# Leaving out semaphore waits that other waits imply, in a planned attention-and-MLP decode kernel

## The chip, the cores and the metric

The kernel runs on one core of a Trainium2 chip. The core has a matrix engine (PE, with a weight-load lane shown as PEld), a vector engine (DVE), an activation engine (ACT), a general-purpose engine (POOL) and a synchronising engine (SP), which here only issues DMA transfers. Each engine works through its own program in order, and the engines meet through semaphores: an instruction can add to a semaphore when it is done, and an instruction can be held until a semaphore has reached a value. The metric is device time in microseconds (us); smaller is better.

## The reference, cut to what matters

Eight sequences decode one token each. The kernel computes a gated sum of an attention branch over the last 2048 cached positions and an MLP branch.

```python
# x: (8, 1, 576); k_cache, v_cache: (8, 16, 8192, 128); all bfloat16
W = 2048
q = (x @ wq).reshape(8, 1, 32, 128).transpose(0, 2, 1, 3)   # 32 query heads
k = repeat(k_cache[:, :, -W:, :], 2, axis=1)                # 16 kv heads, 2 queries each
v = repeat(v_cache[:, :, -W:, :], 2, axis=1)
p = softmax(einsum("bhqd,bhkd->bhqk", q, k) * 128 ** -0.5)
a = einsum("bhqk,bhkd->bhqd", p, v).transpose(0, 2, 1, 3).reshape(8, 1, 4096) @ wo
y = layernorm(x)                                            # no scale, no shift
b = gelu(y @ w1 + b1) @ w2 + b2                             # 576 -> 4608 -> 576
g = sigmoid((x * gate_w).sum(-1, keepdims=True))
out = g * a + (1 - g) * b                                   # (8, 1, 576)
```

## The kernel before

Nearly all the bytes are the two cache windows. They are cut into 32 K units and 32 V units of 2 MB each (one of 8 groups of two kv heads, and a quarter of that group). All big transfers are issued by SP in one fixed order into nine slots of on-chip memory: the two projection weights wq and w1, five K units, then K and V units in turn, with V trailing K by five or six units and one 1.15 MB piece of wo after every eighth V unit. The last in that order are K31, then V26 to V31, the last piece of wo, the bias b2 and the four chunks of w2, the last of them in three pieces. A transfer into a slot waits until the work that read the slot before is done.

What is done with the pieces:

- A K unit is transposed in two halves by DVE (L653). After each half PE adds eight matmuls into four banks of scores (L667; L663 lays down a mask first, once in a group). POOL copies the query columns for it into a block-diagonal operand (L646, names that begin with "qr").
- After a group's fourth K unit comes its softmax. DVE takes the row maximum (L598), moves three of its quarters to the first 32 partitions (L601), combines them (L602, L603, L604) and writes the negated maximum to all four quarters (L607). ACT takes four exponentials (L612), DVE transposes each (L617), sums (L620) and spreads the sums (L621); PE adds them over partitions (L622), and DVE takes the reciprocal (L623) and multiplies in the gate (L629).
- A V unit is 16 matmuls (L690). ACT copies the result out (L696), PE selects the wanted blocks with four fp32 matmuls (L701), and after every second V unit ACT copies the pair out (L711) and POOL scales it (L719).
- After every eighth V unit PE gathers the rows (L734), ACT copies them (L738), and PE multiplies with wo (L552). The products with b2 and w2 go through L552 too. All of L552 adds up in one bank. At the end DVE (L779) and ACT (L780) each copy half of that bank out, and SP and ACT issue the two stores (L782).

The order of the work on each engine is settled before anything runs. Every operation is an `_Op` with a list `deps` of operations that it must wait for. `_Plan.schedule` (from L62) simulates the engines with assumed costs, and from the result writes down one order for each engine; each operation gets its place `pos` in it and its planned start and end, `t0` and `t1`. At the end it adds a wait between neighbouring POOL operations of different kinds (L116 to L121), numbers the transfers on each DMA semaphore, and numbers those operations that somebody waits for (`milestone`).

`_Plan.emit` (from L141) then writes one engine's program. For each dependency of an operation it calls `wait_ge` (L153), unless this engine has already waited for the same semaphore at that value or a higher one; that is the only waiver there is. One wait travels on the instruction itself: the first one called for. Each further wait becomes an instruction of its own ahead of it, holding one or two waits, and shows in the profile as line L153 on the engine's queue (DVEq, ACTq and so on). An operation that has a milestone adds one to its engine's semaphore when it is done.

Of the kernel before, what the change touches and what calls it, by code (L numbers as in the profile page):

```python
# [12 lines left out]
ENGS = ("sp", "act", "pool", "dve", "pe")  # L13
# [25 lines left out]
class _Plan:  # L39
# [22 lines left out]
    def schedule(self):  # L62
        n = len(self.all)
        done = [False] * n
        eng_free = {e: 0.0 for e in ENGS}
        dma_free = 0.0
        remaining = set(range(n))
        npred = [0] * n
        succ = [[] for _ in range(n)]
        for op in self.all:  # L70
            preds = set(d.idx for d in op.deps) | set(d.idx for d in op.after)
            npred[op.idx] = len(preds)
            for p in preds:
                succ[p].append(op.idx)
        ready = [i for i in range(n) if npred[i] == 0]
        count = 0
        while ready:
            best = None
            best_key = None
            for i in ready:  # L80
                op = self.all[i]
                r = 0.0
                for d in op.deps:
                    r = max(r, d.t1 + self.SEM_LAT)
                for d in op.after:
                    r = max(r, d.t0)
                est = max(eng_free[op.eng], r)
                key = (est - 0.2 * op.prio, -op.prio, i)
                if best_key is None or key < best_key:
                    best_key = key  # L90
                    best = i
            op = self.all[best]
            ready.remove(best)
            est = max([eng_free[op.eng]] + [d.t1 + self.SEM_LAT for d in op.deps] + [d.t0 for d in op.after])
            op.t0 = est
            if op.is_dma:
                eng_free[op.eng] = est + op.cost
                if op.nbytes < 65536:
                    op.t1 = est + 0.4 + self.DMA_LAT
                else:  # L100
                    start = max(est + 0.4, dma_free)
                    dma_free = start + op.nbytes / self.DMA_BW
                    op.t1 = dma_free + self.DMA_LAT
            else:
                op.t1 = est + op.cost
                eng_free[op.eng] = op.t1
            op.pos = len(self.order[op.eng])
            self.order[op.eng].append(op)
            done[best] = True
            count += 1  # L110
            for s_ in succ[best]:
                npred[s_] -= 1
                if npred[s_] == 0:
                    ready.append(s_)
        assert count == n, "dependency cycle in plan"
        self.makespan = max(op.t1 for op in self.all)  # L116
        prev = None
        for op in self.order["pool"]:
            narrow = op.name.startswith("qr")
            if prev is not None and narrow != prev.name.startswith("qr"):  # L120
                op.deps.append(prev)  # L121
            prev = op
        cnts = {}
        for e in ENGS:
            for op in self.order[e]:
                if op.is_dma:
                    cnts[op.dma_sem] = cnts.get(op.dma_sem, 0) + 1
                    op.dma_val = 16 * cnts[op.dma_sem]
        needed = set()
        for op in self.all:  # L130
            for d in op.deps:
                if not d.is_dma:
                    needed.add(d.idx)
        for e in ENGS:
            c = 0
            for op in self.order[e]:
                if op.idx in needed:
                    c += 1
                    op.milestone = c
# [713 lines left out]
```

## Time and profile before

| | us |
|---|---|
| median of three runs | 369.81 |
| the three runs | 368.82 to 369.83 |
| the profiled execution: device time | 369.34 |
| the profiled execution: span from first to last instruction | 367.6 |
| PE busy | 268.4 (73%) |
| DVE busy | 212.1 (58%) |
| ACT busy | 48.8 (13%) |
| POOL busy | 42.3 (12%) |

All times of the argument are taken from the one profiled execution. What lies around its span is 369.34 - 367.6 = 1.74 us. Busy shares are means over the whole span. The chain that ended last, which the profile follows back from the last instruction, tells which work set the end at each moment; in it, time called "issue" is time in which an engine waited for nothing that the profile shows, and a name with a q (DVEq, ACTq, POOLq) is an engine's queue handling an instruction that does no arithmetic.

### The profile page before, as it was taken

To read this page: it belongs to the slowest core of one execution; us is meant where nothing else is said; L and a number is where in the kernel's file an instruction comes from. 1 tells how busy PE (TensorE), PEld (TensorE's weight loads), DVE (VectorE), ACT (ScalarE), POOL (GpSimd) and SP (SyncE) were. 2 spreads that over 40 slices of the span, in tenths; PEclk is the share of its full clock that TensorE was granted. 3 is DMA by queue.
4 is the path that set the end of the run, shared out by engine and by line. 5 is a ranking of instruction groups with operands and counts; after the bars stand their busy time and mean duration, and the time that the engine had idled before them with its cause. 6 is when DMAs were issued, how large, how long until landed. Compare 5 with 4: busy or idle time off the path is not lost.

```text
span 367.6 us, 4620 instructions
## 1 busy us (share of the span) xinstructions
PE 268.4 (73%) x1869; PEld 132.4 (36%) x1869; DVE 212.1 (58%) x254; ACT 48.8 (13%) x122; POOL 42.3 (12%) x166
## 2 busy tenths in 40 slices
PE   0349984699598498874986488875987489684887
PEld 0339431244244243332432243322433244232454
DVE  0804599699687764459744754469644874464000
ACT  1010000201300310003000300003000310004110
POOL 8020011012012001010111010010111000000000
PEclk9999998599799878887898878887888788985558
DMA  8999999999999999999999999999999999999993
GB/s 345 428 417 428 430 431 431 431 428 430 428 433 430 425 436 430 428 431 431 431 435 430 420 437 431 427 431 435 428 426 430 437 429 427 426 430 437 421 428 158
DMA packets 11341, 154.62 MB, mean 421 GB/s; under 512 B 1292, under 2 KB 1332, under 8 KB 1976
## 3 DMA queue, kind: packets, MB, share of 16 engines
q1 hardware_dynamic: 11264, 154.29, 98.4%
q8 instruction: 15, 0.25, 0.2%
q10 hardware_dynamic: 56, 0.03, 0.0%
q14 instruction: 6, 0.05, 0.0%
HBM read 154.31 MB, written 0.01 MB: 420 GB/s over the span
## 4 chain that ended last, share of the span: by engine, by line
DMA 58%; PE 20%; DVE 16%; issue 4%; ACT 1%; POOL 1%; SPq 0%; POOLq 0%; DVEq 0%; ACTq 0%
DMA arena<-in_A_k_cache_dram 51%; DVE arena L653 12%; PE ps L667 9%; DMA arena<-in_B_w_dram 7%; PE ps L552 2%; PE ps L509 2%; DVE arena L598 2%; PE ps L690 2%; PE ps L701 2%; PE ps L663 1%; DVE arena L617 1%; PE ps L511 1%; DVE arena L607 0%; DVE arena L601 0%; ACT arena L696 0%
## 5 line engine op out<-in xcount | busy, mean ns | idle before, releaser
L653 DVE STREAM_TRANSPOSE arena<-arena 128x2048 f32<-128x2048 f32 x64 | 145.1, 2296 | 71.8 <-DMA arena<-in_A_k_cache_dram 68.2
L667 PE MATMUL ps<-arena 128*128 128x512 bf16 x512 | 151.7, 453 | 17.2 <-DVE arena L653 17.1
L667 PEld LDWEIGHTS ps<-arena 128*128 128x128 bf16 x512 | 53.8, 112 | 107.0 <-issue 41.1
L646 POOL COPY arena<-arena 32x32 bf16<-32x32 bf16 x128 | 26.0, 203 | 215.4 <-PE ps L667 200.8
L701 PE MATMUL ps<-arena 128*128 128x8 f32 x256 | 37.2, 272 | 15.4 <-ACT arena L696 15.4
L701 PEld LDWEIGHTS ps<-arena 128*128 128x128 f32 x256 | 35.9, 214 | 29.3 <-ACT arena L696 28.0
L696 ACT ACTIVATE arena<-ps 128x512 f32<-128x512 f32 x32 | 19.1, 598 | 191.6 <-PE ps L690 191.6
L663 PE MATMUL ps<-arena 128*128 128x512 bf16 x32 | 14.9, 621 | 33.7 <-DVE arena L617 29.0
L690 PE MATMUL ps<-arena 128*32 128x512 bf16 x512 | 37.1, 413 | 0.7 <-ACT arena L711 0.7
L598 DVE TENSOR_REDUCE arena<-ps 128x1 f32<-128x2048 f32 x8 | 18.3, 2282 | 18.0 <-PE ps L667 18.0
L612 ACT ACTIVATE arena<-ps,arena 128x512 bf16<-128x512 f32 x32 | 21.6, 686 | 41.8 <-DVE arena L607 41.8
L617 DVE STREAM_TRANSPOSE arena<-arena 128x512 bf16<-128x512 bf16 x32 | 19.8, 674 | 0.9 <-ACT arena L612 0.9
L719 POOL TENSOR_TENSOR arena<-arena 128x128 bf16<-128x128 f32 x16 | 8.1, 509 | 91.5 <-ACT arena L711 90.7
L690 PEld LDWEIGHTS ps<-arena 128*32 128x32 bf16 x512 | 11.3, 100 | 18.8 <-issue 12.5
L663 PEld LDWEIGHTS ps<-arena 128*128 128x128 bf16 x32 | 3.5, 127 | 39.4 <-DVE arena L617 35.0
L779 DVE CAST arena<-ps 8x288 bf16<-8x288 f32 x1 | 0.4, 445 | 29.1 <-PE ps L552 29.1
L509 PE MATMUL ps<-arena 128*128 128x8 bf16 x144 | 10.9, 201 | 4.7 <-DMA arena<-in_B_w_dram 4.7
L552 PE MATMUL ps<-arena 128*8 128x288 bf16 (+1 forms) x140 | 12.7, 348 | 1.3 <-ACT arena L738 1.3
L509 PEld LDWEIGHTS ps<-arena 128*128 128x128 bf16 x144 | 10.8, 159 | 5.2 <-DMA arena<-in_B_w_dram 5.2
L623 DVE RECIPROCAL arena<-ps 128x32 f32<-128x32 f32 x8 | 2.9, 358 | 13.4 <-PE ps L622 13.4
L422 PE MATMUL ps<-arena 8*128 8x8 bf16 x8 | 0.5, 167 | 13.5 <-DVE arena L395 9.8
L552 PEld LDWEIGHTS ps<-arena 128*8 128x8 bf16 (+1 forms) x140 | 6.8, 99 | 5.2 <-ACT arena L738 1.8
(88 smaller groups left out, 97.7 us busy)
## 6 DMA issues: line engine op xcount, KB each, us to landing
arena<-in_A_k_cache_dram SPq DMA_DIRECT2D x32, 2048.0 KB, 35.2
arena<-in_A_v_cache_dram SPq DMA_DIRECT2D x32, 2048.0 KB, 36.5
arena<-in_B_w_dram SPq DMA_DIRECT2D x1, 4608.0 KB, 24.2
arena<-in_A_wo_dram SPq DMA_DIRECT2D x4, 1152.0 KB, 35.8
arena<-in_A_wq_dram SPq DMA_DIRECT2D x1, 4096.0 KB, 12.9
arena<-in_B_w_dram SPq DMA_DIRECT2D x3, 1296.0 KB, 33.6
arena<-in_B_w_dram SPq DMA_DIRECT2D x2, 576.0 KB, 28.5
arena<-in_A_wq_dram SPq DMA_DIRECT2D x1, 512.0 KB, 3.3
```

What stands on the lines that cost most here:

```text
L509: ins = e.matmul(out_, lhsT, yT[:, kt, :], start=(kt == 0), stop=False)
L552: ins = e.matmul(ps[32 * j:32 * j + 8, BK_ACC, 0:JN], lhsT, rhs[:, JN * j:JN * j + JN], start=False, stop=True, skip_group_check=True, til ...
L598: mx = add("dve", lambda e: e.tensor_reduce(out=k(MX), in_=ps[:, 0:4, :].rearrange("p a n -> p (a n)"), axis=AXL.X, op=ALU.max), deps=[qk_ ...
L612: return e.activation(out=Pm[:, 512 * c:512 * c + 512], in_=ps[:, c, :], func=ACTF.Exp, bias=k(NB), scale=SCALE, accum_out=k(SUM + c))
L617: pts.append(add("dve", (lambda c=c: lambda e: e.transpose(bass.AP(arena, offset=aoffs("PT") + (g % 2) * 2048 + 128 * c, ap=[[AST, 128], [ ...
L646: return e.tensor_copy(dst, src)
L653: tr = add("dve", (lambda h=h, kb=kb: lambda e: e.transpose(bass.AP(arena_f, offset=foffs("KT") + kb * 2048, ap=[[AST // 2, 128], [1, 2048]]),
L663: mm = e.matmul(ps[:, rc, :], maskL, maskR, start=True, stop=False)
L667: mm = e.matmul(ps[:, rc, :], qbd[:, ub, 2 * h + ee, :], rhs, start=False, stop=(q == 3 and h == 1 and ee == 1))
L690: mm = e.matmul(ps[32 * t:32 * t + 32, BK_OS[i % 2], :], PT[:, g % 2, q, 32 * r4:32 * r4 + 32], slot(s)[:, 512 * r4:512 * r4 + 512], start ...
L696: o_ev[i] = add("act", lambda e: e.activation(out=osb[:, i % 2, :], in_=ps[:, BK_OS[i % 2], :], func=ACTF.Copy), deps=[prev] + ([o_sel[i - ...
L701: mm = e.matmul(ps[:, BK_OS[i % 2], 0:8], osb[:, i % 2, 128 * r:128 * r + 128], i32[:, 8 * r:8 * r + 8], start=(r == 0), stop=(r == 3), sk ...
```

## The change

After the orders are fixed, a new pass goes through the engines' programs and works out for each operation what is known to be done by the time it starts. For every engine and every DMA semaphore it keeps the highest position known to be complete: what the engine's own earlier waits have shown, and what the operations waited for had themselves waited for. A dependency that this knowledge covers already, or that another dependency of the same operation covers, is dropped from `deps`. The ones kept stand in order of planned end, latest first. An engine's own earlier operations count as complete only where a wait has shown it.

The orders of the engines' instructions stay as they were; nothing but waits and semaphore increments differs. In the built programs the instructions that only wait go from 89 to 45 on PE, 49 to 24 on DVE, 35 to 9 on ACT, 30 to 26 on POOL and 35 to 3 on SP (131 fewer in all; each count has the few of the start and the end in it). As fewer operations are waited for, the instructions that increment a semaphore go from 160 to 124 on PE, 258 to 162 on DVE, 98 to 97 on ACT and 166 to 52 on POOL. Because the kept waits are sorted, the wait that travels on the instruction can be another one than before: ahead of some V units it was the wait for the transfer, with the wait for ACT ahead of it, and now it is the wait for ACT, with the transfer's ahead.

```diff
         needed = set()   # in schedule(); the lines below stand ahead of this one
+        key = lambda d: ("dma", d.dma_sem) if d.is_dma else ("eng", d.eng)
+        val = lambda d: d.dma_val if d.is_dma else d.pos + 1
+        last = {e: {} for e in ENGS}
+        heads = {e: 0 for e in ENGS}
+        seen = {}
+
+        def covers(vc, d):
+            return vc.get(key(d), 0) >= val(d)
+
+        left = n
+        while left:
+            for e in ENGS:
+                while heads[e] < len(self.order[e]):
+                    op = self.order[e][heads[e]]
+                    if any(d.idx not in seen for d in op.deps):
+                        break
+                    vc = last[e]
+                    keep = []
+                    for d in sorted(op.deps, key=lambda d: -d.t1):
+                        if covers(vc, d) or (d.eng == e and not d.is_dma and any(covers(seen[o.idx], d) for o in keep)):
+                            continue
+                        if any(covers(seen[o.idx], d) for o in keep):
+                            continue
+                        keep = [o for o in keep if not covers(seen[d.idx], o)] + [d]
+                    op.deps = keep
+                    vc = dict(vc)
+                    for d in keep:
+                        for s_, v in seen[d.idx].items():
+                            vc[s_] = max(vc.get(s_, 0), v)
+                    last[e] = vc
+                    done_vc = dict(vc)
+                    done_vc[key(op)] = max(done_vc.get(key(op), 0), val(op))
+                    seen[op.idx] = done_vc
+                    heads[e] += 1
+                    left -= 1
```

## The prediction

> **What bounds the kernel now.** I began with the page: the span, the granted PE clock, the DMA line and the chain that ended last.
>
> ```profile
> span 367.6 us, 4620 instructions
> PEclk9999998599799878887898878887888788985558
> DMA  8999999999999999999999999999999999999993
> q1 hardware_dynamic: 11264, 154.29, 98.4%
> DMA 58%; PE 20%; DVE 16%; issue 4%; ACT 1%; POOL 1%; SPq 0%; POOLq 0%; DVEq 0%; ACTq 0%
> ```
>
> The DMA engines are busy from the first slice to the last, and no engine's share of the chain comes near theirs. Next I asked for busy times by stretch (columns: length, the engines' busy us, granted PE clock, DMA share, GB/s).
>
> ```profile
> 0.00:20.00 20.00, 4.90 (x131) 4.50 (x132) 7.44 (x30) 1.49 (x2) 8.23 (x22) 1.00 0.92 385
> 20.00:320.00 300.00, 229.41 (x1482) 107.98 (x1478) 192.93 (x203) 39.90 (x101) 32.57 (x141) 0.86 1.01 430
> 320.00:360.00 40.00, 28.91 (x196) 16.64 (x198) 11.28 (x21) 7.04 (x18) 1.53 (x3) 0.60 1.00 428
> 360.00:364.00 4.00, 4.00 (x54) 2.58 (x52) 0.00 (x0) 0.00 (x0) 0.00 (x0) 0.76 0.51 200
> ```
>
> From 20 to 360 us the DMA engines have no gap: share 1.00 to 1.01 at 428 to 430 GB/s. Nothing an engine does in that stretch moves the end unless it leaves DMA without work. How far it is from that, the issues and SP's waits tell.
>
> ```profile
> arena<-in_A_k_cache_dram SPq DMA_DIRECT2D x32, 2048.0 KB, 35.2
> SPq L153 <- DVE arena L653: 168.7, 30, 10.6
> ```
>
> A K unit lands 35.2 us after its issue: some seven units of 2.097 MB / 430 GB/s = 4.9 us stand queued ahead of it. That is the cover for every wait removed before the last K unit.
>
> The place where engines set the end is the tail. This is the chain in order of time (start, length, what), from the last landing it contains:
>
> ```profile
> 282.26 37.04 DMA arena<-in_A_k_cache_dram
> 319.32 2.32 DVE arena L653
> ...
> 329.68 0.15 DVE arena L603
> ...
> 329.92 0.16 DVE arena L604
> 330.08 0.02 issue
> ...
> 330.63 0.16 DVE arena L607
> ...
> 330.89 0.27 ACT arena L612
> ...
> 334.79 0.64 PE ps L622 x2
> 335.43 1.68 PE ps L701 x8
> ...
> 337.13 0.19 ACT arena L711
> 337.32 0.14 issue
> 337.46 1.92 PE ps L690 x16
> ...
> 340.01 0.04 issue
> ...
> 357.54 7.69 PE ps L552 x88
> 365.23 0.03 issue
> ...
> 365.35 0.45 DVE arena L779
> ```
>
> K31 lands at 319.30. After that no landing is waited for: the last softmax runs down to L622 at 334.79, PE takes the last four V units, then the rows of wo, then 88 matmuls of L552 without a break, then the copy-out. DMA is meanwhile ahead. Its next six units (V26 to V31) take 6 x 4.9 = 29.3 us, so V31 lands at about 348.6 (an estimate from the two rates above), while PE, still busy with the units before, takes it up later (at 351.11, in a row below). When the transfers end, and how the clock stands, the tail by microseconds shows:
>
> ```profile
> 361.00:362.00 1.00, 1.00 (x14) 0.55 (x10) 0.00 (x0) 0.00 (x0) 0.00 (x0) 0.55 0.59 236
> 362.00:363.00 1.00, 1.00 (x22) 0.74 (x18) 0.00 (x0) 0.00 (x0) 0.00 (x0) 1.00 0.47 173
> 363.00:364.00 1.00, 1.00 (x22) 0.74 (x18) 0.00 (x0) 0.00 (x0) 0.00 (x0) 1.00 0.11 41
> ```
>
> The last bytes come in soon after 363.0; PE ends at 365.23. The engines trail the transfers by about 2 us, and this is all that a shorter tail can win back. The last piece of w2 has 4 of the 88 matmuls, 4 x 7.69/88 = 0.35 us, so PE can't end before about 363.3 + 0.4 = 363.7, which is 1.5 us earlier than now.
>
> **The change part by part.** It removes instructions that only wait, drops increments, and changes which wait an instruction carries. Orders stay.
>
> SP: 32 waits go, one ahead of most transfers into a slot that a K unit held. Queue depth of 35.2 us covers them: zero. Without that cover a stand-alone wait would be worth about the 0.06 to 0.10 us found below, 32 of them 1.9 to 3.2 us.
>
> PE 44, DVE 25, ACT 26, POOL 4: those before K31's landing lie under a DMA share of 1.01 and cost nothing now. What counts are the hops after 319.30, each read as the gap between the end of the releaser and the start of the next instruction. Two more views are needed for two of them, the tail in order of time:
>
> ```profile
> 330.11 0.67 DVE L607 TENSOR_SCALAR arena<-arena 32x1 f32<-32x1 f32 x4
> 334.79 0.64 PE L622 MATMUL ps<-arena 128*128 128x32 f32 x2 [4.36 <-DVE arena L621]
> 346.38 0.18 ACT L711 ACTIVATE arena<-ps 128x16 f32<-128x16 f32 x1 [1.97 <-PE ps L701]
> 346.71 1.90 PE L690 MATMUL ps<-arena 128*32 128x512 bf16 x16 [0.36 <-ACT arena L711]
> 351.11 1.90 PE L690 MATMUL ps<-arena 128*32 128x512 bf16 x16
> 355.88 0.50 POOL L719 TENSOR_TENSOR arena<-arena 128x128 bf16<-128x128 f32 x1 [8.74 <-ACT arena L711]
> 356.61 0.46 PEld L734 LDWEIGHTS ps<-arena 128*128 128x128 bf16 x8 [1.00 <-POOL arena L719]
> ```
>
> 1. L603 to L604 (m23, t): L603 ends at 329.83, L604 starts at 329.92, with one stand-alone wait between; gap 0.09. L604 to L607, with the wait on the instruction: 330.08 to 330.11, gap 0.03. That wait goes: 0.06.
> 2. L607 to L612, the first exponential: four waits, two instructions plus the carried one; 330.79 to 330.89, gap 0.10. One is left. A carried wait on ACT took 0.02 (PE ends at 337.11, L711 starts at 337.13): 0.08.
> 3. L711 to L690 for V28: 337.32 to 337.46, gap 0.14. Here the wait for ACT stood alone and the instruction carried the transfer's. Now it is the other way round, and the transfer has landed (V28 at about 334). ACT to PE with a carried wait took 0.04 (the issue at 340.01): 0.10.
> 4. The same for V30: 346.56 to 346.71, gap 0.15: 0.10. For V29 and V31 only one wait stands, before and after: 0.
> 5. L719 to L734, the rows of wo: two stand-alone waits holding four, then the carried one; 356.38 to 356.61, gap 0.23. One carried wait remains. Against ACT to PE's 0.04 that is 0.19; against two stand-alone waits at item 1's 0.06 it is 0.12. No row has POOL to PE with one wait; I take 0.17, nearer the end that comes from this gap itself.
> 6. L552 to L779, the copy-out: three stand-alone waits holding six go; 365.23 to 365.35, gap 0.12, against 0.03: 0.09. ACT's half loses its three too.
>
> Sum: 0.06 + 0.08 + 0.10 + 0.10 + 0.17 + 0.09 = 0.60 us. Below nothing: no hop gains a wait, so I see no loss among these. In V units whose transfer is the last to come, the swap of item 3 puts the transfer's wait on an instruction of its own, up to 0.10 us later; these lie before 319 and under DMA.
>
> The increments, 247 fewer: no row prices one. The closest is the spacing of the four L607, each with an increment now: four take 0.67 from 330.11, and the last starts at 330.63, so they start 0.17 apart, and beside a length of 0.14 to 0.16 at most 0.03 apiece is between them. Between zero and three such gaps (0.09), I take zero, as the gap of 0.03 also stands where nothing changes.
>
> The clock, which prices five of the six items: PE stands at half clock through the tail, after an idle of 4.36 us before L622. Items 1 to 5, 0.51 us, make L552 start earlier, at half clock. The clock came back at about 361.9. If it comes back 4.4 us after L552's start, wherever that is, all 0.51 reaches the end. If it comes back at 361.9 whatever PE does, the matmuls gained run at half clock and save their time at full clock, 0.51 x 0.5 = 0.26, and the sum is 0.26 + 0.09 = 0.35. I take the first, since without anything to fix the phase between executions the mean moves by the whole 0.51; 0.35 is the near end of the range.
>
> [...]
>
> [...]
>
> Against which time: the profiled execution took 369.34, and 369.34 - 0.60 = 368.74. The median of the runs is 369.81, 0.47 above it, and the lowest 368.82. I forecast 368.8.
>
> **The rivals.** First, the hops don't shrink: the 0.09 to 0.23 is the semaphore's way between engines and not the waiting instruction. For it: ACT to PE took 0.04 in one place and 0.14 in another, but POOL's end is roughly drawn. Against it: each wide gap has a stand-alone wait in it and each narrow one has none. Time: the mean of the four executions as they stand (three runs and the profiled one), near 369.4.
>
> [...]
>
> Third, on the other side: the clock comes back later in L552. Each us later costs 0.5. Were it full only after the last matmul, the 3.3 us from 361.9 on would take 6.6: 369.34 - 0.60 + 3.3 = 372.0. It decides from 1.7 / 0.5 = 3.4 us later on (1.1 us over the median needs that much beyond the gain of 0.6). [...]
>
> **How the numbers follow.** The forecast, 368.8 with its own range of 368.3 to 369.4 (the sum between 0.35 and 0.69, on executions that differ by 0.5 either way), has 0.55; no change, 369.4, has 0.20; the early clock, 367.8, has 0.17; the late clock 0.08. About 0.3% (1.1 us) is what a measurement of this kernel can tell from no change. Faster than 368.7: the early clock and a third of the forecast, 0.17 + 0.18 = 0.35. Slower than 370.9: 0.08, and 0.02 for runs that drift. The rest, 0.55, is within. The range reaches down to the floor of 367.8 and up to 370.1: the highest run, 369.83, plus 0.3 for no change and a somewhat later clock.
>
> **What would show it.** In the profile after: L604 starts 0.03 after L603's end, L612 0.02 after L607's, L690 of V28 and V30 0.04 after L711's, L734 some 0.06 after L719's, L779 0.03 after the last L552; rows of L153 on DVEq and ACTq are gone from the chain between 319 and 366. DMA share stays 1.00 to 1.01 and K31 lands within 0.5 us of 319.3. L552 starts about 0.5 us sooner after K31's landing (now 38.2). The forecast is wrong if K31's landing itself moves by over 1 us, if the clock in 335 to 357 isn't 0.50, or if it comes back at another time in L552 than about 4.4 us from its start.

## The result, and the profile after

| | before | after |
|---|---|---|
| median | 369.78 us (22 runs) | 368.94 us (22 runs) |
| lowest to highest | 368.79 to 370.94 | 368.24 to 370.56 |
| profiled execution | 369.34 | 368.34 |
| its span | 367.6 | 366.6 |

The ratio after to before is 0.9979, with a 95% interval of 0.9970 to 0.9987: 0.78 us less, between 0.48 and 1.11 (the medians are 0.84 apart). The forecast was 368.8.

In the changed kernel all lines behind the new pass stand 35 lower: L688 is the transpose of before's L653, L702 the scores, L725 the V product, L736 the selection, L746 and L754 the pair's copy and scaling, L769 the rows of wo, L587 the last products, L814 the copy-out.

From the page of the changed kernel: the span, the DMA line, the chain and a K unit's time from issue to landing.

```profile
span 366.6 us, 4489 instructions
DMA  8999999999999999999999999999999999999995
DMA 58%; PE 21%; DVE 14%; issue 3%; ACT 2%; SPq 1%; POOL 1%; POOLq 0%
arena<-in_A_k_cache_dram SPq DMA_DIRECT2D x32, 2048.0 KB, 36.1
```

131 instructions are gone. The transfers' line is as it was but for its last slice, and a unit lands 36.1 us after its issue, not sooner than the 35.2 of before. By stretch (same columns as before):

```profile
20.00:320.00 300.00, 229.93 (x1480) 107.73 (x1478) 192.41 (x203) 39.72 (x100) 32.07 (x140) 0.86 1.01 430
320.00:360.00 40.00, 29.66 (x199) 16.77 (x200) 11.38 (x21) 7.22 (x19) 2.04 (x4) 0.62 1.00 427
```

Where the time went is in the chain from K31's landing on:

```profile
319.41 0.02 issue
...
321.81 5.41 PE ps L702 x16
...
330.30 0.02 issue
330.32 0.16 DVE arena L639
...
331.13 0.02 issue
331.15 0.79 ACT arena L647 x2
...
337.58 0.04 issue
337.62 1.93 PE ps L725 x15
...
356.47 0.05 issue
356.51 0.62 PE ps L769 x8
...
357.44 6.88 PE ps L587 x88
364.31 0.02 issue
364.34 0.45 DVE arena L814
```

K31 lands at 319.41 (before 319.30). The waits on DVEq and ACTq that stood in this chain are gone from it, and every hop forecast to shrink is at 0.02 to 0.06 us. A measure that leaves out what the score matmuls and L587 themselves take is the stretch from the last score matmul (321.81 + 5.41 = 327.22) to the start of L587's run (357.44): 30.22 us. Before, the same chain had

```profile
321.69 5.04 PE ps L667 x16
```

and L552's run at 357.54: 357.54 - 326.73 = 30.81. So the hops gave 0.59 us there and 0.10 at the copy-out.

The two profiled spans differ by 1.0 us, and that is not the hops alone. L587 starts only 0.10 us earlier, since K31 landed 0.11 later and the last scores took 5.41 us for 5.04. Then L587 takes 6.88 us for 7.69, as the clock returns at 360.0, 2.6 us after its start and not 4.4. The tail by microseconds:

```profile
359.00:360.00 1.00, 1.00 (x12) 0.53 (x8) 0.00 (x0) 0.00 (x0) 0.00 (x0) 0.50 1.05 437
360.00:361.00 1.00, 1.00 (x19) 0.72 (x16) 0.00 (x0) 0.00 (x0) 0.00 (x0) 0.98 0.84 339
```

And one row of its timeline, the last weight loads:

```profile
363.88 0.09 PEld L587 LDWEIGHTS ps<-arena 128*8 128x8 bf16 x4 [0.20 <-DMA arena<-in_B_w_dram]
```

This idle time is new: the weight loads stand idle for 0.20 us before the last four matmuls, and a transfer is what ends it. PE itself shows no pause there. In this execution the tail has met the last landing.

### The profile page after: what moved, and what is told of

Its sections match the earlier page's. It is cut to its first block, busy times and chain, and to the rows that moved or that the text cites. A ratio compares the mean times of both kernels' runs of the same rounds, so it can differ in the third digit from the quotient of the medians.

```text
span 366.6 us, 4489 instructions
## 1 busy us (share of the span) xinstructions
PE 268.9 (73%) x1869; PEld 131.8 (36%) x1869; DVE 211.7 (58%) x254; ACT 48.8 (13%) x122; POOL 42.3 (12%) x166
## 4 chain that ended last, share of the span: by engine, by line
DMA 58%; PE 21%; DVE 14%; issue 3%; ACT 2%; SPq 1%; POOL 1%; POOLq 0%
DMA arena<-in_A_k_cache_dram 51%; PE ps L702 10%; DVE arena L688 10%; DMA arena<-in_B_w_dram 7%; PE ps L544 2%; PE ps L587 2%; DVE arena L633 2%; PE ps L725 2%; ACT arena L647 2%; PE ps L736 2%; PE ps L698 2%; DVE arena L652 1%; PE ps L546 1%; DVE arena L642 0%; DVE arena L636 0%
## 5 line engine op out<-in xcount | busy, mean ns | idle before, releaser
L688 DVE STREAM_TRANSPOSE arena<-arena 128x2048 f32<-128x2048 f32 x64 | 144.6, 2293 | 77.4 <-DMA arena<-in_A_k_cache_dram 74.8
L702 PE MATMUL ps<-arena 128*128 128x512 bf16 x512 | 151.3, 452 | 20.8 <-DVE arena L688 20.8
L702 PEld LDWEIGHTS ps<-arena 128*128 128x128 bf16 x512 | 53.6, 111 | 110.4 <-issue 43.2
L736 PE MATMUL ps<-arena 128*128 128x8 f32 x256 | 37.1, 272 | 15.4 <-ACT arena L731 15.4
L736 PEld LDWEIGHTS ps<-arena 128*128 128x128 f32 x256 | 35.8, 213 | 29.3 <-ACT arena L731 28.0
L725 PE MATMUL ps<-arena 128*32 128x512 bf16 x512 | 37.8, 420 | 1.4 <-DMA arena<-in_A_v_cache_dram 0.8
L754 POOL TENSOR_TENSOR arena<-arena 128x128 bf16<-128x128 f32 x16 | 8.1, 508 | 91.7 <-ACT arena L746 91.1
L725 PEld LDWEIGHTS ps<-arena 128*32 128x32 bf16 x512 | 11.3, 101 | 19.8 <-issue 12.0
L814 DVE CAST arena<-ps 8x288 bf16<-8x288 f32 x1 | 0.4, 446 | 27.8 <-PE ps L587 27.8
L587 PE MATMUL ps<-arena 128*8 128x288 bf16 (+1 forms) x140 | 12.8, 349 | 1.3 <-ACT arena L773 1.3
L587 PEld LDWEIGHTS ps<-arena 128*8 128x8 bf16 (+1 forms) x140 | 6.8, 100 | 5.6 <-ACT arena L773 1.8
## 6 DMA issues: line engine op xcount, KB each, us to landing
arena<-in_A_k_cache_dram SPq DMA_DIRECT2D x32, 2048.0 KB, 36.1
```

The source lines that it names most:

```text
L587: ins = e.matmul(ps[32 * j:32 * j + 8, BK_ACC, 0:JN], lhsT, rhs[:, JN * j:JN * j + JN], start=False, stop=True, skip_group_check=True, til ...
L688: tr = add("dve", (lambda h=h, kb=kb: lambda e: e.transpose(bass.AP(arena_f, offset=foffs("KT") + kb * 2048, ap=[[AST // 2, 128], [1, 2048]]),
L702: mm = e.matmul(ps[:, rc, :], qbd[:, ub, 2 * h + ee, :], rhs, start=False, stop=(q == 3 and h == 1 and ee == 1))
L725: mm = e.matmul(ps[32 * t:32 * t + 32, BK_OS[i % 2], :], PT[:, g % 2, q, 32 * r4:32 * r4 + 32], slot(s)[:, 512 * r4:512 * r4 + 512], start ...
L736: mm = e.matmul(ps[:, BK_OS[i % 2], 0:8], osb[:, i % 2, 128 * r:128 * r + 128], i32[:, 8 * r:8 * r + 8], start=(r == 0), stop=(r == 3), sk ...
```

## The experiments

All compare with the kernel before, run on the same chip beside them.

**Which waits carry the gain.** The first two split the change in two: `tail(op)` is true for the operations behind K31's landing. 13 of the 131 waiting instructions go in the first kernel, the other 118 in the second (the expectation's 112 was a miscount).

```diff
                     # first kernel
-                    op.deps = keep
+                    if tail(op):
+                        op.deps = keep
+                    keep = op.deps
                     # second kernel: "if not tail(op)"
```

> Edit: the new pass drops and sorts waits only for the operations that run after K31 has landed (the last softmax, V28 to V31 with what follows them, the last rows of wo, the copy-out); all others keep the waits of before. Theory (the gain is hops of the tail): all of the gain is here, ratio about 0.998 (0.60 us and up to 0.2 more), and from the end of the last score matmul to the start of the last run of L552's matmuls 30.2 us, as in the changed kernel (357.44 - 327.22), where before it was 30.81 (357.54 - 326.73). Rival (the waits of the long stretch matter, 112 of the 131 dropped instructions): ratio 1.000 and the stretch at 30.2 all the same.

> Edit: the reverse, waits are dropped everywhere but for the operations after K31's landing. Theory: nothing, ratio 1.000 within its interval, the stretch from the last score matmul to L552 at 30.8 us, K31 landing at 319.3 to 319.5. Rival (waits of the long stretch): ratio about 0.998, K31 landing earlier by some tenths.

Measured: the tail alone 368.72 us, ratio 0.9973 (0.9959 to 0.9988); all but the tail 369.93 us, ratio 1.0008 (0.9994 to 1.0023). The chains, the tail alone first:

```profile
321.75 5.41 PE ps L711 x16
...
357.39 6.99 PE ps L596 x88
```

```profile
321.80 6.18 PE ps L711 x16
...
331.11 0.02 DVEq L197
...
332.06 0.04 ACTq L197
...
338.58 0.14 issue
...
357.66 0.25 issue
...
358.80 6.65 PE ps L596 x88
```

From the last score matmul to the last run: 357.39 - 327.16 = 30.23 us with the tail's waits gone, 358.80 - 327.98 = 30.82 with all the others gone. The second kernel still has the waiting instructions in its chain and the gaps of 0.14 and 0.25. The two intervals do not overlap. The gain is the tail's, and the rest of the change is worth nothing that shows.

**What an increment costs.** The waits of the changed kernel with the increments of before: the set `needed` is worked out ahead of the new pass.

> Edit: the changed kernel's waits, with every increment of before (247 more). In the changed kernel the four L642 (before L607) took 0.61 us and not 0.67. Theory as predicted (increments cost nothing): ratio to before as the changed kernel's, about 0.998, and the four in 0.61. Rival (an increment has a price on DVE): the four in 0.67 again, the stretch from the last score matmul to L552 at 30.28, and 0.06 us lost of the gain, which the time can't tell.

Measured: 369.63 us, ratio 0.9990 (0.9976 to 1.0005). The four steps L642 (L607 in the kernel before) in this kernel, then in the changed one:

```profile
330.48 0.67 DVE L642 TENSOR_SCALAR arena<-arena 32x1 f32<-32x1 f32 x4
```

```profile
330.50 0.61 DVE L642 TENSOR_SCALAR arena<-arena 32x1 f32<-32x1 f32 x4
```

The rival holds. With the increments back the four take 0.67 us again, and its chain has 327.18 to 357.47, 30.29 us, for 30.22. So three dropped increments on DVE gave 0.06 us here, 0.02 each. Whether the higher median is due to it can't be told: the interval holds the changed kernel's 0.9979 and also 1. In the profiled execution, 369.63, it is nearly all the clock's: there L587 took 8.13 us for 6.88. The changed kernel's 6.88 us had the clock back 2.60 us after the start (360.04 - 357.44), and the 7.69 us of before 4.36 us after it (361.90 - 357.54), 0.46 us more for each us of delay. By that rate the clock came back here some 5.3 us after the start, an estimate.

**Number of waits, or which wait stands alone.** Two kernels put more waits, all long satisfied, ahead of six operations of the tail.

```diff
             # first kernel: eight more, called for after the real ones
+            if op.name in ("t_7", "exp7_0", "pv28", "pv30", "orow3", "fin0"):
+                for v in range(1, 9):
+                    handle.wait_ge(eng_sems["pool" if op.name != "orow3" else "dve"], v)
             inst = op.fn(handle)
             # second kernel: one more, called for first, so that it travels on the instruction
+            if op.name in ("t_7", "exp7_0", "pv28", "pv30", "orow3", "fin0"):
+                handle.wait_ge(eng_sems["pool" if op.name != "orow3" else "dve"], 1)
             for d in op.deps:
```

> Edit: the changed kernel, with eight more waits ahead of six operations of the tail (the last of the four maximum steps, the first exponential, V28, V30, the rows of wo, DVE's half of the copy-out). All eight have long been satisfied, and the wait that comes last still travels on the instruction. Theory refined (not the number of waits costs, but whether the wait that comes last stands alone): the four extra instructions are run through while the engine waits anyway; the gaps stay at 0.02 to 0.06 us (0.04 for V28 and V30, 0.06 for the rows of wo, 0.03 for the copy-out), only ahead of the maximum step, whose predecessor lasts 0.14 us, may some of their time show. Rival (each waiting instruction has its price wherever it stands): each gap longer by 4 x 0.05 to 0.10, that is 0.2 to 0.4 us, together 1.2 us or more.

> Edit: the changed kernel, with one more wait, long satisfied, called for first ahead of the same six operations, so that this one travels on the instruction and the wait that comes last stands alone in front: one waiting instruction more at four places, two at V28 and V30 as before (one with both waits). Theory refined: the gaps are those of the kernel before, 0.09 at the maximum step, 0.10 at the exponential, 0.14 at V28 and V30, some 0.15 at the rows of wo (0.23 before, with two in a row), some 0.10 at the copy-out; the stretch from the last score matmul to L552 30.2 + 0.43 = 30.6 us. Rival (the gain came from the number of waits or of increments): the gaps stay as in the changed kernel, 30.2.

One execution each: 368.70 us with eight more waits, 369.91 us with one. The chains; first eight more:

```profile
330.25 0.05 DVEq L192
...
330.44 0.16 DVE arena L642
...
331.25 0.02 issue
...
337.71 0.04 issue
...
356.60 0.05 issue
...
364.60 0.02 issue
```

Then one more, called for first:

```profile
330.45 0.02 DVEq L190
...
331.34 0.02 ACTq L190
...
337.61 0.32 issue
337.93 1.92 PE ps L727 x16
...
356.82 0.14 issue
...
357.86 8.04 PE ps L589 x88
365.90 0.03 issue
```

With eight more, the gaps are those of the changed kernel: 0.02 at the exponential, 0.04 at V28, 0.05 at the rows of wo, 0.02 at the copy-out. Only the last maximum step (L642 here, L639 in the changed kernel), whose predecessor is done in 0.14 us, waits visibly: of its four waiting instructions, 0.05 us each, two are still to come when the predecessor ends, and it starts 0.24 after that end and not 0.02. The stretch is 357.56 - 327.19 = 30.37 us. With a single wait more, the wide gaps are back, since the wait that comes last now stands alone: 0.09 at the maximum step and the exponential, 0.10 at V28 (ACT's copy is done at 337.83), 0.14 at the rows of wo, 0.09 at the copy-out. The stretch is 327.34 to 357.86, 30.52 us, against 30.6 expected. So the price is not the number of waits. A waiting instruction whose wait was over before its turn ran while the engine waited anyway (four gaps of 0.02 to 0.05 us with four more of them); one that held the last wait made the gap 0.06 to 0.09 us longer than in the changed kernel. The 1.2 us between the two times is mostly not this: the last 88 matmuls took 8.04 us here and 7.03 with eight more, for the clock came back, estimated at the same rate, 5.1 us after their start and not 2.9. The gaps are read inside one trace each and don't hang on the times.

**The stream's cover.** The same trick on everything from K0 to K30 (233 more waiting instructions, the expectation's 187 being a miscount; 61 on SP as it says).

```diff
+            if op.name.startswith(("tr", "qk", "qr", "dk", "dv", "pv", "ovac", "osel", "oev", "oT", "d_wo")) and op.deps and op.t0 < self.t_last:
+                handle.wait_ge(eng_sems["pool"], 1)
```

> Edit: the changed kernel, with the same trick on every transfer, transpose, score and value product, selection and copy-out of K0 to K30 and their V units (187 more waiting instructions on the five engines, 61 of them on SP), the tail left alone. Theory (queued transfers cover the stream): each hop of the stream 0.06 to 0.10 us longer, K31's landing at 319.3 to 319.5, and the ratio to before the changed kernel's, 0.998. Rival (hops in the stream reach the end): K31's landing later by up to 32 x 0.1 = 3 us, ratio above 1.000.

Measured: 369.30 us, ratio 0.9986 (0.9973 to 0.9998). Its chain:

```profile
319.56 0.02 issue
...
321.96 5.41 PE ps L705 x16
...
357.60 7.01 PE ps L590 x88
```

The trick did lengthen the hops: in the stream the first selection matmul of a V unit starts 0.14 us after ACT's copy, for 0.05 in the changed kernel. Still K31 lands at 319.56, 0.15 us after the changed kernel's and far from the rival's 3 us; the kernel with one more wait in the tail alone, its stream unchanged, had 319.54. The stretch of the tail is 357.60 - 327.37 = 30.23. The queue hides the 233 waiting instructions more as it hid the 118 dropped ones. The interval holds the changed kernel's 0.9979 and leaves out the rival's ratio above 1.

**The clock, and the floor behind it.** The changed kernel and the kernel before, each with 60 matmuls put into PE's pause ahead of the last softmax's sum.

```diff
+        def warm_fn(e):
+            mm = None
+            for _ in range(60):
+                mm = e.matmul(ps[:, BK_S, 256:384], ident, maskR[:, 0:128], start=True, stop=True, skip_group_check=True)
+            return mm
         # its operation stands on PE just ahead of "sum_pe7"
```

> Edit: the changed kernel, with 60 matmuls of 128x128 added on PE between the product of V27 and the sum of the last softmax (4.1 us of idle time), written to 128 columns of a bank that nothing else uses; they are extra work. Theory (the clock is lost in this pause, and the transfers are a floor): the granted clock stays at 1.00 from 331 on, PE catches up with the transfers, L552 ends at the last landing, and the time is at the floor in every run, 368.2 or a little less; ratio to before 0.995 to 0.997, spread of the runs below 0.4 us. Rival (the pauses of 0.7 us for ACT keep the clock at half whatever happens in the pause): granted clock 0.50 from about 340 on, ratio 0.998 or above. If the matmuls last longer than the pause, the last softmax's sum starts later by as much.

> Edit: the kernel before, all its waits kept, with the same 60 added matmuls in the pause of the last softmax (extra work). Theory (the end is the later of the engines' tail and the last landing): with the pause filled PE catches up with the transfers, waits for them again at V29, V31 and w2, and the 0.6 us of the hops is hidden: time 368.3 with a spread below 0.5 us, as the changed kernel with the same matmuls, so that leaving the waits out is worth nothing there. Rival (the hops are additive): 368.29 + 0.6 = 368.9.

Measured: on the changed kernel 368.29 us (368.24 to 368.53 over 5 runs), ratio 0.9962 (0.9950 to 0.9974). On the kernel before 368.47 us (368.31 to 369.63 over 12 runs, nine of them at 368.65 or less), ratio 0.9971 (0.9960 to 0.9983). The timeline of the first (start, length, what, idle time before and what ended it), and its clock:

```profile
330.32 3.52 PE L836 MATMUL ps<-arena 128*128 128x128 bf16 x60
...
339.01 1.90 PE L738 MATMUL ps<-arena 128*32 128x512 bf16 x16 [0.70 <-DMA arena<-in_A_v_cache_dram]
...
360.90 2.03 PE L600 MATMUL ps<-arena 128*8 128x288 bf16 x26 [0.86 <-DMA arena<-in_B_w_dram]
```

```profile
335.00:336.00 1.00, 0.73 (x13) 0.33 (x16) 0.06 (x1) 0.18 (x1) 0.51 (x1) 1.00 0.88 377
...
338.00:339.00 1.00, 0.30 (x2) 0.21 (x1) 0.00 (x0) 0.00 (x0) 0.00 (x0) 0.50 0.87 360
```

The clock holds through the pause but not, as the theory had it, to the end: it goes to half at about 338, in the short pauses that the rival named. What was won by then is enough. PE has caught up with the transfers, waits for V29, V30 and V31 (0.70, 0.62 and 0.28 us) and for pieces of w2, and the end is the last landing plus the last matmuls. Not all of its lead is the filling's: in this execution the clock was full from 320 on (its mean of 0.74 over 320 to 358 is accounted for by the half clock from 337.9 on), so the last scores, too, ran at full clock and ended at 325.95, 1.3 us sooner than in the changed kernel. On the kernel before the same filling reaches nearly the same time although all its waits are there: 0.18 us between the medians, against 0.84 without the filling. So the dropped waits are worth little once PE no longer trails the transfers. That they are worth nothing there isn't shown: three of its twelve runs stayed at 369.42 to 369.63, against the expected spread below 0.5 us, and none of the changed kernel's five did. The profiled execution of that kernel is its slowest, 369.63: there the last scores took 6.57 us, at half clock until 327.7, the filling began at 332.01, and PE still trailed.

The changed kernel with the filling has the lowest median of all and, over five runs, the smallest spread.

## Why the prediction was right

**The transfers bound the stream, so the waits dropped there cost nothing.** Shown: no gain that the time can tell with 118 instructions fewer (1.0008), K31 at 319.56 with 233 more.

**The six hops.** Predicted and measured, from the two chains (item 5 from the tail in order of time):

| item | gap before | after | predicted gain | measured |
|---|---|---|---|---|
| 1, maximum step | 0.09 | 0.02 | 0.06 | 0.07 |
| 2, exponential | 0.10 | 0.02 | 0.08 | 0.08 |
| 3, V28 | 0.14 | 0.04 | 0.10 | 0.10 |
| 4, V30 | 0.15 | 0.05 | 0.10 | 0.10 |
| 5, rows of wo | 0.23 | 0.06 | 0.17 | 0.17 |
| 6, copy-out | 0.12 | 0.02 | 0.09 | 0.10 |

Rows of V30 and the rows of wo in the changed kernel:

```profile
346.54 0.18 ACT L746 ACTIVATE arena<-ps 128x16 f32<-128x16 f32 x1 [1.97 <-PE ps L736]
346.78 1.90 PE L725 MATMUL ps<-arena 128*32 128x512 bf16 x16 [0.27 <-ACT arena L746]
355.95 0.50 POOL L754 TENSOR_TENSOR arena<-arena 128x128 bf16<-128x128 f32 x1 [8.63 <-ACT arena L746]
356.51 0.45 PEld L769 LDWEIGHTS ps<-arena 128*128 128x128 bf16 x8 [0.84 <-POOL arena L754]
```

Sum 0.62, and the forecast 0.60. The step that failed is the increments, "Between zero and three such gaps (0.09), I take zero": they gave 0.06 on the four negations. With it the tail's hops gave 0.68 us (0.59 + 0.10 by the chains); the medians differ by 0.84, and the interval, 0.48 to 1.11, holds both.

**The time.** That 368.8 came so near to 368.94 is partly luck. It was counted from the profiled execution's 369.34, which lies 0.44 us under the median of the 22 runs, and the medians moved by 0.84 and not by 0.60; the two nearly cancel. What the runs bear out is the difference: 0.60 lies within the interval.

**The clock.** One of the forecast's own signs of being wrong came true: the clock came back 2.6 us after L587's start in the changed kernel and not 4.4, and at 360.0, not 361.9. So neither of the two cases that the prediction weighed is what the traces show. They show a grid. In the changed kernel the granted clock changes at 322.50, 325.91, 332.74 and 360.04, which are 1, 2 and 8 times 3.41 us apart; in the kernel before at 320.94, 324.35, 331.18 and 361.90, 1, 2 and 9 times. The row of before that places the second of these changes:

```profile
324.00:325.00 1.00, 1.00 (x6) 0.37 (x4) 0.00 (x0) 0.00 (x0) 0.00 (x0) 0.82 1.03 442
```

The clock of the two filled kernels keeps to such a grid where its rows place the changes: 337.9 and 358.4 on the changed kernel, 6 times 3.41 us apart, 327.7 and 338.0 on the kernel before, 3 times. And the grid lies differently against the kernel, in the changed kernel 1.56 us later than before (322.50 - 320.94). How late the clock came back counted as the third rival had it: 0.46 us of L587 for each us, near half a us. By this rate the shortest run of these 88 matmuls without a pause, 6.65 us with all but the tail's waits left out, had the clock back some 2.1 us after its start, and the longest, 8.13 us, some 5.3, both estimates.

What holds is the reason for counting items 1 to 5 in full: the grid was not at a fixed place between these executions, and so a start that is 0.51 us sooner is, as an estimate, 0.51 us on the mean, though not in one execution. The fixed moment, with the measured sizes 0.59 / 2 + 0.10 = 0.40 us, lies below the interval.

In the two profiled executions the clock gave 0.81 us in L587 and took 0.37 in the last scores, 0.44 together, and the hops gave 0.69; K31 landed 0.11 later. The check "L552 starts about 0.5 us sooner after K31's landing" came out at 0.2 (38.24 to 38.03) because of these 0.37. The stretch between the two pieces that the clock changed was the measure to name.

The 3.41 us at whose end the clock came back in the changed kernel, 356.63 to 360.04, have a pause of 0.3 us in them (ahead of 357.44).

**The floor** was set at 363.7 for PE's end, with the end of the traffic at about 363.3 as the last landing. The last landing is later. The chain of the changed kernel with the filling has it at 333.02 + 30.98 = 364.00:

```profile
333.02 30.98 DMA arena<-in_B_w_dram
...
364.05 0.43 PE ps L600 x4
```

PE's end is 364.48 there, in the slowest of the five runs (368.53), and 364.32 in the changed kernel, whose last four matmuls met their landing. So there were some 0.9 us to win on the kernel before (365.23 - 364.32), not 1.5, and the early clock's 367.8 was out of reach: no run of any kernel here is below 368.19, and the changed kernel's fastest runs and the filled ones pile up at 368.2 to 368.5.

**The rivals.** That the hops don't shrink fell with the chains. No run shows the early clock that the chances give 0.17, at 367.8: in the changed kernel the clock was at half from 332.74 to 360.04, and with the pause filled it held to 337.9 and the median was 368.29. The late clock over all of L552 was in no profile here: the longest run of these 88 matmuls without a pause was 8.13 us, in the kernel with the old increments.

**Waits and increments on DVE.** Item 1 and the increments stand between operations of DVE, while at item 6 DVE waits for PE. A waiting instruction with the last wait cost 0.07 us at item 1, and an increment 0.02 between operations of 0.14.

## What to carry to other kernels

Count the waits only where no queue covers them: here 13 of 131 dropped instructions, those behind the last awaited landing, made the whole gain. There, see to it that the wait that comes last travels on the instruction itself; satisfied waits ahead of it cost nothing where the engine would wait anyway (with eight more of them the gaps stayed at 0.02 to 0.05 us). Before shaving hops of a tail, look whether PE's clock has gone to half in an idle pause, as here at 331.18 in the one of 4.36 us ahead of L622: filling that pause brought the kernel before, with all its waits, 1.3 us at the median (369.81 to 368.47), nearly to the floor that the transfers set, though in three of twelve runs it stayed about 1 us above. And where a gain is smaller than what the clock moves from one execution to the next, read it in a stretch of the trace in which no matmul of the chain runs across a change of the clock, and take the time over many runs.

## What the runs showed that was not expected

Increments were not free between very short DVE operations: four of 0.14 us took 0.67 us with an increment each and 0.61 with one. And work that is the same in each kernel varied with the moment the clock came back: the last scores between 5.04 and 6.57 us (some 4.2 in the filled kernel with full clock, an estimate: they ended at 325.95, and with DVE's transposes done at 323.91, as in the kernel with eight more waits, they will have begun at about 321.78 as there) and the last 88 matmuls between 6.65 and 8.13. With PE kept busy in its one long pause five runs of the changed kernel spread over 0.29 us, where without it 22 spread over 2.3; so few runs can't show how far the spread would go, and twelve of the kernel before with the filling spread over 1.3.
